# First chunk of an mLSTM and GCU kernel: the weights' bounds on GpSimd, and the first fading ahead of w_out's second pair

## The chip, the core and the metric

The kernel runs on one core of a Trainium2 chip. A core has a matrix engine (TensorE, "PE" in the profile; "PEld" is its loading of weights), three engines for elementwise work (VectorE "DVE", ScalarE "ACT", GpSimd "POOL"), a sync engine that issues transfers (SyncE "SP"), and 16 DMA engines. Each engine works through its own queue in order; between engines the order is kept by semaphores. TensorE writes to PSUM; the other operands lie in SBUF, 128 partitions wide. The metric is the device time of one execution, in microseconds; lower is better.

## What is computed

An mLSTM cell (batch 4, 8 heads, 768 steps, head size 40) gives x, 3072 tokens of 320 numbers; then a feed-forward with a cosine gate:

```python
for t in range(S):
    m_new = np.maximum(f_gate[:, :, t] + m, i_gate[:, :, t])
    f_stab = np.exp(f_gate[:, :, t] + m - m_new)
    i_stab = np.exp(i_gate[:, :, t] - m_new)
    m = m_new
    C = f_stab[..., None, None] * C + i_stab[..., None, None] * np.einsum('bhd,bhe->bhde', vt, kt)
    n = f_stab[..., None] * n + i_stab[..., None] * kt
    h_tilde = np.einsum('bhde,bhe->bhd', C, qt)
    denom = np.maximum(np.abs(np.einsum('bhd,bhd->bh', n, qt)[..., None]), 1.0)
    y[:, :, t] = 1.0 / (1.0 + np.exp(-o_gate[:, :, t])) * h_tilde / denom
x = y.transpose(0, 2, 1, 3).reshape(B * S, H * D)
h = x @ w_in                 # w_in 320 x 2048, float64
out = (h * np.cos(h)) @ w_out   # w_out 2048 x 320, float64; out is float32
```

The two weight matrices come as 64-bit floats, and the kernel turns them into 32-bit floats itself, by arithmetic on their bits.

## The kernel before

**Cells.** Time is cut into 6 chunks of 128 steps. A *cell* n = 4c + b is chunk c of batch b: the scores of keys and queries (`scores`, PE L530), their weighing with the decay (`weigh`, DVE L536), the values (`values`, PE L556 to L565), and the recurrent state st, which each cell first fades (`fade`, four POOL instructions, L650) and then increments (`state`, four DVE instructions, L692). The state is read by the values of the same cell before it is faded. The decay of a cell comes from a mask on POOL (`decay_exponents`, L434) and eight exponentials on ACT (`decay`, L448).

**Feed-forward.** It runs one chunk behind the cells, in eight blocks f2 of 2 x 128 columns of w_in. A block multiplies (`Up`, PE L715 and L709) into two PSUM banks "pup"; ACT rounds (`near`, L723), DVE subtracts (`rest`, L726), ACT takes the sine (`sin`, L731), DVE multiplies (`gate`, L735), which frees the banks for the next block. `down` (PE L829) multiplies the gated block with a *pair* of row blocks of w_out and sums up over the blocks in PSUM; it stands one block later in PE's queue.

**Conversion of the weights.** It lies wholly in the time up to and in the feed-forward's first chunk (c = 0). w_in comes in four *quarters* of three *pieces* each: two of 128 x 512 (here i0 and i1) and one of 128 x 256 (the *last*, for the tile w_in_l). w_out comes in eight *pairs* of 128 x 640, pair 0 to pair 7. For each piece or pair:

- `take_apart`, ACT: L167 makes the magnitude of the high word a float, L169 scales the low word for the rounding;
- `bound`, DVE: L173 limits the magnitude to a least and a greatest value, two operations in one instruction; L174 shifts its bits left by 5 and right by 2;
- `join`, DVE, L183: sets sign and top bit from the high word;
- `round_up`, POOL, L187: adds the low word's share.

`on_vector(made)` issues, for a list of such pieces, first all `bound`s, then all `join`s (of the first of the list last), then all `round_up`s.

**Where it stands.** The order of all queues is written out by hand. The first cells (n = 0 to 3) are done by `first_cells`, which also converts w_in's first quarter. `first_period` is cell 4 (n = B) with blocks 0 and 1 and converts pair 0, the second quarter, and pair 1. Then `both_parts(0, b)` for b = 1, 2, 3 does cells 5, 6, 7 with blocks 2b and 2b + 1. In its half i = 0 it takes apart a pair and up to two pieces (three from b = 2), converts the first two of them before `down_slot`, fades the state after the values, and converts the rest behind the fading; in its half i = 1 it converts a further pair, and at b = 1 one piece before it. In `first_period` the conversion of pair 1 (`on_vector([piece])`) stands ahead of `fade(n)` and `state(n)`.

A buffer of four quarters (`quarter()`) takes the words of w_in, three buffers `bits` those of w_out. SP's loads into them wait until the `round_up` of the piece that had the buffer before is done.

Of the kernel before, what the change touches and what calls it, by code (L numbers as in the profile page):

```python
# [16 lines left out]
OP = mybir.AluOpType  # L17
# [3 lines left out]
LEAST, GREATEST = (struct.unpack("f", struct.pack("I", b))[0] for b in (0x38000000, 0x47EFFFFF))  # L21
# [8 lines left out]
def kernel(  # L30
# [20 lines left out]
    nc = tc.nc  # L51
# [111 lines left out]
    def take_apart(dst, bits):  # L163
        n = dst.shape[1]
        hi, lo = bits[:, 0:n, 1], bits[:, 0:n, 0].bitcast(U32)

        nc.scalar.activation(out=dst, in_=hi.bitcast(FP), func=AF.Abs)  # L167

        nc.scalar.activation(out=bits[:, 0:n, 0], in_=lo, func=AF.Copy, scale=2.0 ** -29)  # L169

    def bound(dst):
        t = dst.bitcast(I32)
        nc.vector.tensor_scalar(out=dst, in0=dst, scalar1=LEAST, scalar2=GREATEST, op0=OP.max, op1=OP.min)  # L173
        nc.vector.tensor_scalar(out=t, in0=t, scalar1=5, scalar2=2, op0=OP.logical_shift_left,  # L174
                                op1=OP.logical_shift_right)

# [12 lines left out]
    def on_vector(made):  # L189

        for dst, bits in made:
            bound(dst)
        for dst, bits in (*made[1:], *made[0:1]):
            join(dst, bits)
        for dst, bits in made:
            round_up(dst, bits)
# [379 lines left out]
    def denominators(n):  # L576

        K = C // 32
        if n == B:
            d = p2.tile([128, K, 32], FP, name="dt", tag="dt")  # L580
        else:
            d = heads_of[n][:, 3].rearrange("q (k i) -> q k i", k=K)
        nc.vector.transpose(out=d, in_=heads_of[n][:, 2].rearrange("q (t k) -> q k t", t=32))
        dn = dns[n] = p2.tile([128, K, 2], FP, name="d2", tag="d2")
        both = d[:, :, FROM0:FROM1 + 1:FROM1 - FROM0]
        nc.vector.scalar_tensor_tensor(out=dn, in0=both, scalar=-TWO_PI, in1=least.rearrange("q (k g) -> q k g", g=2), op0=OP.mult, op1=OP.max)
        nc.vector.scalar_tensor_tensor(out=dn, in0=both, scalar=TWO_PI, in1=dn, op0=OP.mult, op1=OP.max)
        if n > B:
            dns[n] = d[:, :, 0:2]
        nc.vector.reciprocal(out=dns[n], in_=dn)  # L590
# [608 lines left out]
    def first_period():  # L1199
        n = B  # L1200
        up = Up(0, 0)
        scores(n)
        warm(8, psum_o())
        for e in range(2):
            up.near(e)
        for e in range(2):
            up.rest(e)
        weigh(n)
        for e in range(2):
            up.sin(e)  # L1210
            up.gate(e)
        values(n)
        seam(n)
        p, piece = outs.pop(0)
        take_apart(*piece)
        low_dimensions(n + 1)
        for some in pieces:
            take_apart(*some)
        out_of_psum(n)
        on_vector([piece])  # L1220
        up = Up(0, 1)
        turn_blocks(n + 1)
        on_vector(pieces)
        pieces.clear()
        more = weights_in(2)
        pieces.append(next(more))
        load_M(n + 2)
        pieces.extend(more)
        load_blocks(n + 2)
        load_out(p)  # L1230
        for e in range(2):
            up.near(e)
        for e in range(2):
            up.rest(e)
        for e in range(2):
            up.sin(e)
            up.gate(e)
        p, piece = outs.pop(0)
        take_apart(*piece)
        denominators(n)  # L1240
        on_vector([piece])
        fade(n)
        state(n)
        decay_exponents(n + 1)
        odd_values_of(n + 1)
        down_slot(0, 1)
        sigmoid(1)
        decay(n + 1)
        divide(n)
        scale_q(n + 1)  # L1250
        weigh_k(n + 1)
        load_G(n + 2)
        load_two(n + 2)
        load_out(p)
        load_M(n + 3)
# [6 lines left out]
    def both_parts(c, b):  # L1262

        n = (c + 1) * B + b
        cell = n < N
        for i in range(2):
            f2 = 2 * b + i
            up = Up(c, f2)
            if cell and i == 0:
                scores(n)  # L1270
            if cell and i == 1:
                if n % 2 == 1 and n > B + 1 and n + 3 < N:
                    load_two(n + 3)
            for e in range(2):
                up.near(e)
            for e in range(2):
                up.rest(e)
            if i == 0:
                if cell:
                    weigh(n)  # L1280
                    if n + 1 < N:
                        decay_exponents(n + 1)
                for e in range(2):
                    up.sin(e)
                    up.gate(e)
                if (c, b) == (0, 1):
                    seam_out(B)
                if c > 0:
                    sums(c, f2)
                if b == 0 and c == 1:  # L1290
                    sigmoid(c + 1)

                if c == 0:
                    p, piece = outs.pop(0)
                    made = [piece, *(pieces.pop(0) for _ in range(min(2 if b < 2 else 3, len(pieces))))]
                    for dst, bits in made:
                        take_apart(dst, bits)
                    on_vector(made[0:2])
                    load_out(p)
                    if b + 2 < B:  # L1300
                        load_blocks(n + 2)
                    if n in (B + 1, B + 2):
                        low_dimensions(n + 1)
                if c > 0 and cell and n + 1 < N:
                    decay(n + 1)
            else:
                if cell:
                    seam_out(n)
                if cell:
                    state(n)  # L1310
                for e in range(2):
                    up.sin(e)
                    up.gate(e)
                if c > 0:
                    sums(c, f2)
                if c == 0:
                    p, piece = outs.pop(0)
                    made = [*([pieces.pop(0)] if b == 1 else ()), piece]
                    for dst, bits in made:
                        take_apart(dst, bits)  # L1320
                    decay(n + 1)
                    sin_next()
                    on_vector(made[0:-1])
                    turn_blocks(n + 1, "k")
                    on_vector(made[-1:])
                if cell and n + 1 < N:
                    if c > 0:
                        weigh_k(n + 1)
                    odd_values(n + 1)
            down_slot(c, f2)  # L1330
            if cell and i == 0:
                values(n)
                seam(n)
                normalize_turned(n)
                fade(n)
                if c == 1 and b < 3:
                    weight_sums(b + 1)
                if n > B + 1 and n + 2 < N:
                    load_blocks(n + 2)
                if n > B + 1 and n + 3 < N:  # L1340
                    load_E(n + 3)
                if b == B - 2 and c + 2 < NC:
                    load_o(c + 2)
                if c == 0:
                    on_vector(made[2:])
                    if b + 2 < B:
                        pieces.extend(weights_in(b + 2))
                if c > 0:
                    sin_next()
            if i == 1:  # L1350
                if c == 0 and b + 2 < B:
                    load_two((n + 3) // 2 * 2)
                    load_E(n + 3)
                if c == 0:
                    turn_blocks(n + 1, "q")
                    scale_q(n + 1)
                    weigh_k(n + 1)
                    load_out(p)
                elif cell and n + 1 < N:
                    turn_blocks(n + 1)  # L1360
                    if n + 1 < (fast + 1) * B:
                        scale_q(n + 1)
                if b == B - 1 and c == fast - 1:
                    sigmoid(c + 2)
                if (c, f2) == (0, LAST):
                    weight_sums(0)
                if c == fast - 1 and b > 0:
                    up_weight_sums(b - 1)
                if c == fast - 1 and b == B - 1:
                    x_sums(c + 1)  # L1370
# [139 lines left out]
```

## Time and profile before

| what | value |
|---|---|
| three runs | 516.17, 517.38, 517.54 us; median 517.38 us |
| the profiled execution | 517.38 us; its span from the first to the last instruction is 515.5 us |
| granted clock of TensorE | 0.999 of full speed |
| busy in 60:80 us of the span | PE 17.90, DVE 15.97, ACT 14.73, POOL 13.15 us of 20 |
| busy in 80:90 us | PE 8.08, DVE 8.20, ACT 9.05, POOL 6.06 us of 10 |
| busy in 90:100 us | PE 10.00, DVE 9.69, ACT 7.17, POOL 5.27 us of 10 |
| L173, 128x640 / 128x512 / 128x256 on DVE | 480 / 464 / 337 ns each |
| L187, 128x640 / 128x512 / 128x256 on POOL | 1564 / 1309 / 745 ns each |

Times in the profile are microseconds from the start of the span, mean durations of one instruction nanoseconds. A row of the timeline has the start, the duration, the engine, the line, the operation, output and input with their shapes, how many instructions the row stands for, and in brackets how long the engine stood idle before it and what ended that. A row of the waits has the engine and line that waited, the engine, tile and line it waited for, and the microseconds in all, how often, and the longest. The first cells end, and cell 4 with the feed-forward's first block begins, at some 38 us; the second cell's values (b = 1) stand at 70 us, the third's (b = 2) at 94 us, the fourth's (b = 3) at 115.5 us; c = 0 ends at some 140 us.

### The profile page before, as it was taken

Reading aid. Unit: us, or ns where it says so; the run is one execution under the profiler, and the core shown is the slowest. Engines: PE = TensorE matmul, PEld = TensorE weight load, DVE = VectorE, ACT = ScalarE, POOL = GpSimd, SP = SyncE. Lnnn points to the kernel's source line nnn. Section 1 sums busy time; section 2 is a strip of 40 time slices with the busy share of each in tenths; the row PEclk is TensorE's granted clock in tenths of the full one; section 3 lists DMA queues with packets and bytes.
Section 4 is the critical chain, followed back from the end, with each engine's and each line's share of the span. In section 5 each row is a group of like instructions: output and inputs, shape, how many; then the busy total and the mean of one; then the engine's idle time right before and its main releaser. Section 6 shows DMA issues by size and latency. Waiting matters only on the chain.

```text
span 515.5 us, 11095 instructions
## 1 busy us (share of the span) xinstructions
PE 499.2 (97%) x4038; PEld 377.1 (73%) x4038; DVE 417.7 (81%) x839; ACT 326.4 (63%) x618; POOL 300.9 (58%) x387
## 2 busy tenths in 40 slices
PE   6999898999999999999999999999999999999997
PEld 3874454655666677778878778878878878687876
DVE  4799788988778888789987989988979867677655
ACT  2889787685945547748658867557867554443541
POOL 7525556553934855858566869656768454535340
PEclk9999999999999999999999999999999999999999
DMA  9979989998167337305728204937202000010001
GB/s 136 217 194 250 261 184 270 184 229 170 27 193 144 117 85 139 93 32 167 178 71 163 71 31 143 190 85 160 72 32 79 7 6 4 3 53 0 1 0 53
DMA packets 100903, 57.87 MB, mean 112 GB/s; under 512 B 63520, under 2 KB 93312, under 8 KB 100848
## 3 DMA queue, kind: packets, MB, share of 16 engines
q1 hardware_dynamic: 97696, 55.48, 45.9%
q10 hardware_dynamic: 2752, 1.23, 0.9%
q8 instruction: 32, 0.52, 0.4%
q0 software_dynamic: 400, 0.44, 0.3%
q14 instruction: 23, 0.19, 0.1%
HBM read 51.71 MB, written 4.11 MB: 108 GB/s over the span
## 4 chain that ended last, share of the span: by engine, by line
PE 72%; DVE 8%; DMA 6%; POOL 4%; ACT 3%; issue 3%; SPq 3%; DVEq 0%; POOLq 0%; ACTq 0%
PE acc L979 23%; PE pup L783 16%; PE pup L715 6%; PE pup L799 6%; PE late L979 4%; PE ps L530 3%; PE po L829 3%; DMA G<-G_d 2%; PE pup L709 2%; DMA blocks<-in_moe_w_in_dram 2%; PE vt L565 2%; DMA qr<-in_q_dram 2%; PE vt L556 2%; DVE t L508 1%; PE pw L1061 1%
## 5 line engine op out<-in xcount | busy, mean ns | idle before, releaser
L723 ACT ACTIVATE n<-pup 128x512 int32<-128x512 f32 x64 | 37.0, 594 | 97.6 <-DVE pup L808 65.0
L731 ACT ACTIVATE n<-n 128x512 f32<-128x512 f32 x96 | 58.2, 627 | 21.6 <-DVE n L726 15.9
L818 POOL TENSOR_TENSOR g<-g,n 128x512 f32<-128x512 f32 x31 | 39.5, 1276 | 51.4 <-ACT n L731 47.3
L726 DVE SCALAR_TENSOR_TENSOR n<-pup,n 128x512 f32<-128x512 f32 x64 | 43.1, 689 | 22.3 <-ACT n L723 19.7
L715 PE MATMUL pup<-xT,w_in_sb 128*128 128x512 f32 x128 | 58.8, 602 | 1.9 <-DVE g L735 1.7
L979 PE MATMUL acc<-w_out_sb,g 128*128 128x160 f32 x320 | 58.4, 302 | 0.0
L800 POOL TENSOR_TENSOR blocks<-blocks 128x256 f32<-128x256 f32 x32 | 25.6, 799 | 53.2 <-ACT blocks L792 53.1
L979 PE MATMUL acc<-T,g 128*128 128x160 f32 x304 | 55.8, 301 | 0.0
L448 ACT ACTIVATE E<-E,tab 128x128 f32<-128x128 f32 x160 | 50.2, 391 | 5.6 <-POOL E L434 5.4
L783 PE MATMUL pup<-xT,w_in_sb 128*128 128x256 f32 x192 | 53.1, 385 | 0.3 <-ACT blocks L792 0.2
L979 PEld LDWEIGHTS acc<-w_out_sb,g 128*128 128x128 f32 x320 | 48.9, 190 | 4.5 <-issue 2.7
L735 DVE TENSOR_TENSOR g<-pup,n 128x512 f32<-128x512 f32 x64 | 42.6, 687 | 6.1 <-ACT n L731 5.6
L715 PEld LDWEIGHTS pup<-xT,w_in_sb 128*128 128x128 f32 x128 | 23.0, 189 | 33.0 <-issue 31.2
L979 PEld LDWEIGHTS acc<-T,g 128*128 128x128 f32 x304 | 46.1, 190 | 0.9 <-issue 0.4
L783 PEld LDWEIGHTS pup<-xT,w_in_sb 128*128 128x128 f32 x192 | 33.8, 189 | 9.6 <-ACT blocks L792 5.9
L808 DVE TENSOR_TENSOR pup<-pup,blocks 128x256 f32<-128x256 f32 x32 | 13.9, 435 | 30.7 <-PE pup L799 27.5
L783 PE MATMUL pup<-x_room,room 128*128 128x256 f32 x128 | 38.2, 380 | 0.0
L791 ACT COPY blocks<-pup 128x512 f32<-128x512 f32 x32 | 18.6, 581 | 29.6 <-PE pup L783 27.8
L829 PE MATMUL po<-w_out_sb,g 128*128 128x320 f32 x128 | 36.3, 436 | 0.1
L979 PE MATMUL acc<-T,blocks 128*128 128x160 f32 x160 | 36.2, 308 | 0.0
L799 PE MATMUL pup<-xL,w_in_l 64*128 64x512 f32 x128 | 36.1, 641 | 0.0
L512 POOL TENSOR_TENSOR qG<-t,G 128x512 f32<-128x512 f32 x20 | 25.9, 1296 | 17.1 <-DVE t L508 16.9
(214 smaller groups left out, 1220.4 us busy)
## 6 DMA issues: line engine op xcount, KB each, us to landing
E<-M_d SPq DMA_DIRECT2D x21, 512.0 KB
qr<-in_q_dram SPq DMA_DIRECT2D x72, 80.0 KB
kr<-in_k_dram SPq DMA_DIRECT2D x72, 80.0 KB
bits<-in_moe_w_out_dram SPq DMA_DIRECT2D x8, 640.0 KB
G<-G_d SPq DMA_DIRECT2D x18, 256.0 KB
blocks<-in_moe_w_in_dram SPq DMA_DIRECT2D x32, 128.0 KB
out_dram<-o_sb SPq DMA_DIRECT2D x23, 160.0 KB
o<-in_o_gate_dram SPq DMA_DIRECT2D x40, 80.0 KB
```

The costliest lines, as they stand in the source:

```text
L448: nc.scalar.activation(out=Es[n][:, h], in_=Es[n][:, h], func=AF.Exp, scale=-1.0, bias=tab[:, c, 0, g:g + 1])
L512: nc.gpsimd.tensor_tensor(out=qG, in0=qkT[n][0], in1=Gs[n], op=OP.mult)
L715: nc.tensor.matmul(pu.rearrange("p (b t) -> p b t", b=B), w_in_sb[:, i, ts(2 * f2 + e, 128)], xT[c][:, i:NK * B:NK], start=(i == 0 and not ...
L723: nc.scalar.activation(out=self.n[e], in_=self.pu[e], func=AF.Copy, bias=0.25)
L726: nc.vector.scalar_tensor_tensor(out=self.n[e].bitcast(FP), in0=self.pu[e], scalar=0.25, in1=self.n[e], op0=OP.add, op1=OP.subtract)
L731: nc.scalar.activation(out=r, in_=r, func=AF.Sin, scale=TWO_PI_DOWN)
L735: nc.vector.tensor_tensor(out=g, in0=self.pu[e], in1=self.n[e].bitcast(FP), op=OP.mult)
L783: nc.tensor.matmul(bank[:, part].rearrange("p (b t) -> p b t", b=B // 2), w[:, f2], x, start=start, stop=stop, skip_group_check=True)
L799: nc.tensor.matmul(pu, w_in_l[r, f2], xL[c][r].rearrange("p b t -> p (b t)"), start=False, stop=True, skip_group_check=True)
L818: tt(out=self.g, in0=self.g, in1=self.n[e].bitcast(FP), op=OP.mult)
L829: nc.tensor.matmul(po[c][b], gs[c, f][:, ts(b, C)], w_out_sb[:, f], start=(f == 0), stop=(f == NF - 1))
L979: nc.tensor.matmul(a, lhs, rhs, start=start, stop=stop)
```

## The change

`bound` is taken in two: the limiting of the magnitude (L173) and the shift (L174), which is now `shift_out`. A new function `bounded_apart` issues `take_apart` on ACT and then the limiting on POOL. In `first_period` and in `both_parts` for c = 0 it takes the place of `take_apart`, and `on_vector` issues only the shift on DVE. The limiting thus stands in POOL's queue where `take_apart` stood in ACT's: ahead of the `round_up`s of all pieces that were taken apart together. A fourth piece (`made[3:]`, at b = 2) is taken apart and limited later, behind the fading. `first_cells` keeps `bound` on DVE for the first quarter. In `first_period`, `fade(n)` moves ahead of `on_vector([piece])` of pair 1, whose limiting still stands ahead of the fading.

```diff
     def bound(dst):
+        nc.vector.tensor_scalar(out=dst, in0=dst, scalar1=LEAST, scalar2=GREATEST, op0=OP.max, op1=OP.min)
+        shift_out(dst)
+
+    def bounded_apart(dst, bits):
+
+        take_apart(dst, bits)
+        nc.gpsimd.tensor_scalar(out=dst, in0=dst, scalar1=LEAST, scalar2=GREATEST, op0=OP.max, op1=OP.min)
+
+    def shift_out(dst):
         t = dst.bitcast(I32)
-        nc.vector.tensor_scalar(out=dst, in0=dst, scalar1=LEAST, scalar2=GREATEST, op0=OP.max, op1=OP.min)
         nc.vector.tensor_scalar(out=t, in0=t, scalar1=5, scalar2=2, op0=OP.logical_shift_left,
                                 op1=OP.logical_shift_right)
@@ on_vector
         for dst, bits in made:
-            bound(dst)
+            shift_out(dst)
@@ first_period
         p, piece = outs.pop(0)
-        take_apart(*piece)
+        bounded_apart(*piece)
         low_dimensions(n + 1)
         for some in pieces:
-            take_apart(*some)
+            bounded_apart(*some)
         out_of_psum(n)
         on_vector([piece])
...
         p, piece = outs.pop(0)
-        take_apart(*piece)
+        bounded_apart(*piece)
         denominators(n)
+        fade(n)
         on_vector([piece])
-        fade(n)
         state(n)
@@ both_parts
-                    for dst, bits in made:
-                        take_apart(dst, bits)
+                    for dst, bits in made[0:3]:
+                        bounded_apart(dst, bits)
                     on_vector(made[0:2])
...
                     for dst, bits in made:
-                        take_apart(dst, bits)
+                        bounded_apart(dst, bits)
                     decay(n + 1)
...
                 if c == 0:
+                    for dst, bits in made[3:]:
+                        bounded_apart(dst, bits)
                     on_vector(made[2:])
```

## The prediction

> **What bounds the kernel now.** First the page's busy time, which says who could be the bound, then the waits of the matrix engine (PE) in 40:215, where the change lies.
>
> ```profile
> span 515.5 us, 11095 instructions
> PE 499.2 (97%) x4038; PEld 377.1 (73%) x4038; DVE 417.7 (81%) x839; ACT 326.4 (63%) x618; POOL 300.9 (58%) x387
> ...
> PE ps L530 <- DVE st L692: 1.9, 1, 1.9
> PE pup L715 <- DVE g L735: 1.7, 2, 1.4
> PE ps L530 <- DVE t L508: 0.5, 1, 0.5
> ```
>
> PE is busy 97%: from 106 us on it hardly rests (10.00 of each 10 us up to 200), so any shift that PE has at 106 lasts to the end, and all that can be won in the first chunk is about 4 us: 1.9 (fading and state late), 1.7 (gates late), 0.5 (transposes late). Losses have no such limit. Next the timeline of 47:84, for the order in which these come about.
>
> ```profile
> 47.83 0.49 DVE L173 TENSOR_SCALAR w_out_sb<-w_out_sb 128x640 f32<-128x640 f32 x1
> 49.85 1.58 POOL L187 TENSOR_TENSOR w_out_sb<-w_out_sb,bits 128x640 int32<-128x640 int32 x1 [5.29 <-ACT kr L485]
> 52.08 0.47 ACT L167 ACTIVATE w_in_l<-blocks 128x256 f32<-128x256 f32 x1
> 53.00 3.39 PE L829 MATMUL po<-w_out_sb,g 128*128 128x320 f32 x12
> 55.21 1.28 DVE L726 SCALAR_TENSOR_TENSOR n<-pup,n 128x512 f32<-128x512 f32 x2
> 55.42 2.56 POOL L187 TENSOR_TENSOR w_in_sb<-w_in_sb,blocks 128x512 int32<-128x512 int32 x2 [3.99 <-DMA o<-in_o_gate_dram]
> 61.02 1.56 POOL L187 TENSOR_TENSOR w_out_sb<-w_out_sb,bits 128x640 int32<-128x640 int32 x1 [2.34 <-issue]
> 62.54 1.38 POOL L650 TENSOR_TENSOR st<-st,tab 40x128 f32<-40x128 f32 x4
> 63.99 1.09 POOL L434 TENSOR_SCALAR_AFFINE_SELECT E<-E 128x1024 f32<-128x1024 f32 x1
> 64.23 1.16 PE L530 MATMUL ps<-t,t 40*128 40x128 f32 x14 [1.86 <-DVE st L692]
> 82.27 1.29 DVE L735 TENSOR_TENSOR g<-pup,n 128x512 f32<-128x512 f32 x2
> 83.11 1.10 PE L715 MATMUL pup<-xT,w_in_sb 128*128 128x512 f32 x2 [1.39 <-DVE g L735]
> ```
>
> To be seen: POOL rounds up w_out's pair 0 at 49.85, 1.6 us before PE multiplies by it (53.00). The fading (L650) stands behind pair 1's rounding up, and PE waits 1.86 us for the state that follows it. And POOL's L187 mostly runs beside DVE work on PSUM (L726, L735) or transposes.
>
> The last view, the timeline of 38:42, shows what happens where it does not:
>
> ```profile
> 38.52 1.41 POOL L187 TENSOR_TENSOR w_in_sb<-w_in_sb,blocks 128x512 int32<-128x512 int32 x1 [2.08 <-DMA vs<-in_v_dram]
> 38.82 1.26 DVE L174 TENSOR_SCALAR w_in_l<-w_in_l 128x256 int32<-128x256 int32 x1
> 39.88 1.15 POOL L434 TENSOR_SCALAR_AFFINE_SELECT E<-E 128x1024 f32<-128x1024 f32 x1
> 40.11 1.19 DVE L183 SCALAR_TENSOR_TENSOR w_in_l<-blocks,w_in_l 128x256 int32<-128x256 int32 x1
> ```
>
> The same L174 takes 0.29 at 53.46, the same L183 0.42 at 54.27. Beside a POOL instruction each lasts until POOL's ends, and POOL's next one lets DVE go first: the engines take turns, one instruction each. This concerns the shift (L174) and the join (L183), both with SBUF operands only.
>
> The Trainium skill ("SBUF — State Buffer", Who interferes with whom) has this as an exclusive lock on a port pair, held for a whole instruction against a DVE operation in a two-port mode or with two SBUF inputs; the rows agree. It speaks against the change: without it the sum below would be the first rival's.
>
> **Price of a bound on POOL.** No two-operation TENSOR_SCALAR runs on POOL in the trace. Nearest row with one input: AFFINE_SELECT, 1112 ns at 1024 columns and 293 ns at 128, so 0.91 ns a column: 0.76 us for 640, 0.64 for 512, 0.41 for 256. Below: MEMSET, 621 ns at 640, 418 at 384, 737 at 768, so 0.62/0.52/0.31. Above: L187, two inputs, 1.56/1.31/0.75. I take AFFINE_SELECT, as it too reads one tensor and writes one. In all 17 instructions move (8 of w_out, 6+3 of w_in): DVE loses 8 x 0.48 + 6 x 0.42 + 3 x 0.29 = 7.2 us (L173 where no POOL instruction lies beside it), POOL gains 8 x 0.76 + 6 x 0.64 + 3 x 0.41 = 11.1 us. After 106 us both lie under PE.
>
> **First period (a).** POOL's queue now has pair 0's bound, the three bounds of w_in's second quarter (i0, i1, last), and only then pair 0's rounding up. The last bound waits for ACT's L167, which ends at 52.55; with 0.41 the rounding up can't start before 53.0 nor end before 54.55. That alone is 1.6 us on PE, which stands at 53.00 with nothing else queued. Turns add to it. DVE: pair 0's shift at 48.65 (bound 47.85 to 48.61) in place of 48.36, so the transposes end at 52.0. Bound i1 holds to 52.33, shift i0 to 52.75, bound last to 53.16, shift i1 to 53.6, rounding up of pair 0 to 55.15, shift last to 55.45, joins (0.61+0.34+0.68) to 57.1. So PE's L829 goes from 53.0 to 55.2 (+2.2), and DVE's L726 from 55.21 to 57.1 (+1.9), with gates and L167 of pair 1 (57.85 to 59.7) behind it.
>
> **First period (b), the fading.** Rounding up the quarter (55.42 to 58.68, 3.26 long) ends at 57.1+3.26 = 60.4. Then bound of pair 1 to 61.15, and the fading, now ahead, from 61.15. The shift (0.49) and join (0.82) of pair 1 fall into its four instructions, so it ends near 63.5, the state near 64.5. PE's L530, shifted by 2.2 from 61.99, would come at 64.2: the 1.86 us are used up by (a), and the scores end 0.3 later than before. What is late next is the mask L434: 60.4 + 0.76 + 1.38 + 1.56 + turns 0.49 + 0.82 = 65.4 against 63.99, +1.4. Queued behind it are eight exponentials (65.12 before), L723, L726, the weighing L536 and PE's L556, which came at 70.04 just behind the weighing (69.29, first half 0.68) and L829. So +1.4 for PE. DMA issues on POOL (L674) move along; SP's loads wait for buffers that come free as much later as PE runs, and I add nothing.
>
> **Second cell (b = 1).** From the end of the gates at 71.77 (T): bounds at T, T+1.3 and, for i1, T+2.4, each behind its L167. Shift i0 ends at T+2.4, where bound i1 competes with the join: join of pair 2 ends at T+4.5, T+3.6 before. Taken out later is i1's L173 (0.58) less a turn: L726 at 80.18 comes 0.5 later, so the gate and PE's L715 (83.11, which waits for it) too. Behind it last's shift waits 0.7 for bound of pair 3 (cover: L173s of 0.29 and 0.48 gone), +0.1 at 88.36. Together +0.6.
>
> **Third cell (b = 2).** PE has slack up to 105.48. The last piece's bound is put behind the fading (99.69, 1.70 long). Join of pair 4 ends 0.4 later by the same competition; rounding up 1.56+1.30, fading, bound 0.41, and then shift, two joins: L726 at 103.3, 102.55 before; L735 and PE's L715 +0.7. Fourth cell: two bounds of pairs, rounding up at 117.25 for use at 122.43, cover 3.6 us; nothing.
>
> **Sum**: 1.4 + 0.6 + 0.7 = +2.7. The profiled execution took 517.38 (span 515.5 and 1.9 around it), which is also the median of the runs; 517.4 + 2.7 = **520.1**. With the low price each stage loses some 0.3 less (519.2). With the high one: in (a) the rounding up ends at 56.3 and the joins at 58.2, L434 starts at 67.3 (+3.3); second cell: bounds end at T+4.2, joins T+5.7, less 0.6: +1.5; third +2.0: 524.2.
>
> A page's figure: the Trainium skill ("GPSIMD Engine Reference", Performance versus the Vector engine) puts a one-input body of at most two operations at 1.03 cycles an element, by which an estimate of 640 columns at 1.2 GHz is 0.55 us without dispatch; it would lie near the low price.
>
> **Rivals.** *Faster, by turns that cost nothing*: the bounds run in POOL's gaps (idle 44.6 to 49.85 and 51.4 to 55.4) and DVE's shifts and joins keep their 0.43 and 0.69. Then pair 0's rounding up ends at 54.6 (PE +1.6), the fading at 60.4, the 1.86 is gone (-0.3), and DVE, lighter by 1.5 us from 71.77 on, takes the 1.39 at 83.11 and the 0.53 at 88.36: -2.2, 515.2. For: the gaps are there, and L692 and L726 are not held. Against: the rows at 38.82 and 40.11. It decides if L726 of the second block comes no later than 55.5. *No change*: turns cost only half, and (a) is paid for by the 1.86 and half of DVE's relief: 517.4. *Dear bounds*: 524.2, for: POOL's two-input rows; against: AFFINE_SELECT and COPY. That the bounds don't move is excluded by the changed program's queues: 17 L173 are gone from DVE and stand on POOL.
>
> **How the numbers follow.** Forecast 0.50 (519.0 to 521.5), faster 0.20, no change 0.15, dear 0.15. Within 0.3% is +-1.55 us, about what a measurement of this kernel can tell from none. Faster 0.20, same 0.15, slower 0.65. The range runs from the faster rival's time to the dear bounds': 515.2 to 524.2.
>
> **What would show it.** POOL's TENSOR_SCALAR of 640 columns near 0.76 us where alone; PE's first L829 at about 55 with a wait for POOL; the wait of L530 for the state gone; shifts and joins with means above 0.43 and 0.69; a mask at 65.4; PE's wait for g at 83 and 105 kept or longer. Wrong, if L829 comes near 54.6 and DVE's L726 at 55.2, or if the wait at 83 vanishes.

## The result, and the profile after

| | before | after |
|---|---|---|
| median | 517.41 us (4 runs, 516.17 to 517.54) | 529.71 us (4 runs, 528.23 to 530.96) |
| ratio, 95% interval | | 1.0242 [1.0205, 1.0279] |
| profiled execution, its span | 517.38, 515.5 us | 530.77, 529.0 us |

The change makes the kernel 2.4% slower, some 12.3 us, where 2.7 us were forecast; 529.7 lies outside the range. First the page of the kernel after, its span and busy times:

```profile
span 529.0 us, 11092 instructions
PE 505.5 (96%) x4038; PEld 382.0 (72%) x4038; DVE 418.3 (79%) x822; ACT 326.5 (62%) x618; POOL 335.1 (63%) x404
```

VectorE has 17 instructions fewer and is no less busy (418.3 us, 417.7 before): its shifts alone grew from 9.5 to 14.1 us (w_out, w_in and last pieces together), probably because some of them now lie beside GpSimd's work. GpSimd has 17 more and 34.2 us more busy time, 2.0 us for each new instruction. The groups by form (line, engine, operation, shapes, count, then busy time and mean ns of one, then the idle time before them and what ended it) show the new instruction, now L178, and two that answer to it, the shift L182 and the down L837:

```profile
L178 POOL TENSOR_SCALAR w_out_sb<-w_out_sb 128x640 f32<-128x640 f32 x8 | 18.8, 2345 | 9.0 <-ACT w_out_sb L167 5.4 <-DVE g L743 3.4
L178 POOL TENSOR_SCALAR w_in_l<-w_in_l 128x256 f32<-128x256 f32 x3 | 3.2, 1065 | 0.1
L182 DVE TENSOR_SCALAR w_out_sb<-w_out_sb 128x640 int32<-128x640 int32 x8 | 5.5, 683 | 11.9 <-POOL w_out_sb L178 11.9
L837 PE MATMUL po<-w_out_sb,g 128*128 128x320 f32 x128 | 40.5, 474 | 7.0 <-POOL w_out_sb L195 7.0
```

To be seen: a bound of 640 columns lasts 2.35 us on GpSimd (0.48 on VectorE), one of 256 columns 1.07 us; the shifts of w_out wait 11.9 us for bounds, and the downs wait 7.0 us for w_out's rounding up (L195), for which they waited 0.1 us before. The waits of TensorE in 40:230 us:

```profile
PE po L837 <- POOL w_out_sb L195: 7.0, 2, 4.1
PE pup L723 <- DVE g L743: 2.5, 2, 1.7
PE ps L538 <- DVE t L516: 1.5, 2, 1.1
PE pup L717 <- POOL w_in_l L195: 0.9, 2, 0.6
```

The forecast's one certain gain is there: the 1.9 us for the state are gone from this list. But the wait of the second row, for the gates, has grown (2.5, and 1.7 in the same stretch of the kernel before, 40:215), as has that for the transposes (1.5, 0.5 before) and for w_in (0.9, 0.3 before), and a new one of 7.0 us stands at the top. Where its two parts arise, from the timeline (44:72 us, and the last row from the second cell):

```profile
49.79 2.36 POOL L178 TENSOR_SCALAR w_out_sb<-w_out_sb 128x640 f32<-128x640 f32 x1 [3.37 <-ACT w_out_sb L167]
...
52.45 4.04 POOL L178 TENSOR_SCALAR w_in_sb<-w_in_sb 128x512 f32<-128x512 f32 x2 [0.30 <-ACT w_in_sb L167]
...
56.46 1.06 POOL L178 TENSOR_SCALAR w_in_l<-w_in_l 128x256 f32<-128x256 f32 x1
...
57.49 1.55 POOL L195 TENSOR_TENSOR w_out_sb<-w_out_sb,bits 128x640 int32<-128x640 int32 x1
57.55 1.64 DVE L182 TENSOR_SCALAR w_in_l<-w_in_l 128x256 int32<-128x256 int32 x1 [0.42 <-POOL w_in_l L178]
...
59.09 7.37 PE L837 MATMUL po<-w_out_sb,g 128*128 128x320 f32 x16 [4.05 <-POOL w_out_sb L195]
...
86.27 4.57 PE L837 MATMUL po<-w_out_sb,g 128*128 128x320 f32 x16 [2.96 <-POOL w_out_sb L195]
```

Read GpSimd's rows downwards: pair 0's bound ends at 52.15, and its shift and join on VectorE take 1.6 us more. But the three bounds of w_in's quarter stand between in GpSimd's queue and take 5.1 us; the rounding up starts at 57.49, and TensorE, which has nothing else queued, waits 4.05 us. The shift of the last piece (57.55), 0.29 us where nothing lies beside it, lasts 1.64, until just after the rounding up ends (59.04).

One thing in these times is not the change's. In this profile the granted clock of TensorE fell to 0.50 in 25:30 us, where both kernels' programs are the same, and the first cell's values stand at 48.13 in place of 46.26. These 1.9 us belong to that execution: the same dip is in three of the profiles below, that of the kernel before with its fading moved among them. (In these four profiles the first cell's values stand at 48.13 to 48.26, in the eight others, that of the kernel before among them, at 45.23 to 46.57.) Less this dip, the later points of the timeline stand behind before's as follows: first down +4.2 us, values of b = 1 +4.4, values of b = 2 +9.6, end of the span +11.6. So the first period costs 4.4 us, the second cell 5.2, the third 2.0, and what TensorE has lost by then it keeps to the end. The 12.3 us between the medians have part of this dip in them; by this profile the change itself costs some 11.6.

### The profile page after: what moved, and what is told of

Read it like the earlier page. It is cut to its first block, busy times and chain, and to the rows that moved or that the text cites. A ratio compares the mean times of both kernels' runs of the same rounds, so it can differ in the third digit from the quotient of the medians.

```text
span 529.0 us, 11092 instructions
## 1 busy us (share of the span) xinstructions
PE 505.5 (96%) x4038; PEld 382.0 (72%) x4038; DVE 418.3 (79%) x822; ACT 326.5 (62%) x618; POOL 335.1 (63%) x404
## 4 chain that ended last, share of the span: by engine, by line
PE 64%; DMA 10%; POOL 8%; SPq 5%; ACT 4%; DVE 4%; issue 4%; ACTq 0%; DVEq 0%; POOLq 0%
PE acc L987 21%; PE pup L791 15%; PE pup L723 6%; PE pup L807 5%; PE late L987 4%; DMA E<-M_d 3%; PE po L837 3%; PE ps L538 2%; DMA blocks<-in_moe_w_in_dram 2%; PE pup L717 2%; PE vt L573 2%; DMA vs<-in_v_dram 2%; PE vt L564 2%; POOL w_in_sb L178 1%; SPq L381 1%
## 5 line engine op out<-in xcount | busy, mean ns | idle before, releaser
L723 PE MATMUL pup<-xT,w_in_sb 128*128 128x512 f32 x128 | 58.8, 602 | 2.8 <-DVE g L743 2.5
L734 DVE SCALAR_TENSOR_TENSOR n<-pup,n 128x512 f32<-128x512 f32 x64 | 43.1, 689 | 19.6 <-ACT n L731 17.2
L723 PEld LDWEIGHTS pup<-xT,w_in_sb 128*128 128x128 f32 x128 | 23.1, 190 | 33.6 <-issue 28.9
L837 PE MATMUL po<-w_out_sb,g 128*128 128x320 f32 x128 | 40.5, 474 | 7.0 <-POOL w_out_sb L195 7.0
L837 PEld LDWEIGHTS po<-w_out_sb,g 128*128 128x128 f32 x128 | 26.3, 209 | 20.8 <-POOL w_out_sb L195 8.7
```

Source lines behind the costliest of these rows:

```text
L723: nc.tensor.matmul(pu.rearrange("p (b t) -> p b t", b=B), w_in_sb[:, i, ts(2 * f2 + e, 128)], xT[c][:, i:NK * B:NK], start=(i == 0 and not ...
L734: nc.vector.scalar_tensor_tensor(out=self.n[e].bitcast(FP), in0=self.pu[e], scalar=0.25, in1=self.n[e], op0=OP.add, op1=OP.subtract)
L837: nc.tensor.matmul(po[c][b], gs[c, f][:, ts(b, C)], w_out_sb[:, f], start=(f == 0), stop=(f == NF - 1))
```

## Experiments

The times of the kernel before in the four series were 516.84, 516.86, 516.73 and 516.93 us; each ratio is against its own series.

### What a bound costs on GpSimd, alone

A kernel of its own, with none of the model's work: tiles of 128 to 1024 columns, two instructions of each kind in a row on GpSimd (the loops are shortened here).

```diff
+for n in (128, 256, 512, 640, 1024):
+    g.tensor_scalar(out=a[:, 0:n], in0=a[:, 0:n], scalar1=0.25, scalar2=4.0, op0=OP.max, op1=OP.min)
+for n in (256, 640):
+    g.tensor_scalar(out=a[:, 0:n], in0=a[:, 0:n], scalar1=0.25, scalar2=None, op0=OP.max)
+    g.tensor_scalar(out=a[:, 0:n], in0=a[:, 0:n], scalar1=1.0, scalar2=0.0, op0=OP.mult, op1=OP.add)
+    g.tensor_tensor(out=a[:, 0:n], in0=a[:, 0:n], in1=b[:, 0:n], op=OP.add)
+    g.tensor_copy(out=a[:, 0:n], in_=b[:, 0:n])
```

> A kernel that computes nothing of the reference: it runs rows of single GpSimd instructions alone, then six bounds of 640 columns beside six shifts on VectorE; its output is left at zero but for one copied row block. Price theory: the bound with maximum and minimum takes 3.3 ns a column plus about 0.2 us (from 2.35 us at 640 and 1.07 at 256 in the changed kernel) also where it runs alone, so 0.64, 1.07, 1.9, 2.35 and 3.6 us at 128, 256, 512, 640, 1024; one operation instead of two about half of the slope. Rival, contention: alone it takes near 0.76 us at 640 as AFFINE_SELECT's rows give, and only beside VectorE's work 2.35.

Groups by form of this kernel (L27 max and min, L30 max alone, L33 multiply and add):

```profile
L27 POOL TENSOR_SCALAR a<-a 128x640 f32<-128x640 f32 x2 | 4.7, 2340 | 0.2
...
L30 POOL TENSOR_SCALAR a<-a 128x640 f32<-128x640 f32 x2 | 3.6, 1804 | 0.2
...
L33 POOL TENSOR_SCALAR a<-a 128x640 f32<-128x640 f32 x2 | 1.4, 724 | 0.2
```

The 2.34 us are the price of the operation itself, with VectorE idle: the same form of instruction with multiply and add takes 0.72 us, and so does a copy. (From one start to the next it is 2.43 against 0.81 us.) From 256 to 640 columns max and min cost (2340 - 1061) / 384 = 3.33 ns a column, max alone (1804 - 846) / 384 = 2.5, multiply and add (724 - 404) / 384 = 0.83. The Trainium skill ("GPSIMD Engine Reference", Performance versus the Vector engine) gives one rate for bodies of up to two operations, 1.03 cycles an element, and calls one-input work roughly line-rate (Engine selection); multiply and add and the copy agree, maximum and minimum don't, and the measurement decides.

A second part was to set six bounds beside six shifts. The shifts ran much earlier than these bounds, so that it says nothing of turns; these are measured below.

### The same queue, a quarter of the columns

```diff
-        nc.gpsimd.tensor_scalar(out=dst, in0=dst, ...)
+        part = dst[:, 0:dst.shape[1] // 4]
+        nc.gpsimd.tensor_scalar(out=part, in0=part, ...)
```

> The changed kernel with the bound on GpSimd done on the first quarter of each piece's columns only (three quarters of the limiting are left out), all else in place. Price theory: a bound of 160 columns takes about 0.74 us, the price that the prediction took for 640, so the time is near the predicted 520.1 (518.5 to 522). Rival, place: what costs is that the bounds stand ahead of the roundings in GpSimd's queue and take turns with VectorE, whatever their length: 525 or more.

517.55 us (10 runs), ratio 1.0013 [0.9998, 1.0028]. Three quarters of each piece's limiting are left out. A bound of 160 columns lasts 745 ns, nearly what the prediction assumed for 640, and in place of +2.7 us there are +0.7 (-0.1 to +1.4). That is far from the rival's 525, but also below the 518.5 to 522 that were expected from the price. So a wrong price is not the whole of it: at the assumed price the sum was too large.

### No bounds at all

```diff
-        nc.gpsimd.tensor_scalar(out=dst, in0=dst, scalar1=LEAST, scalar2=GREATEST, op0=OP.max, op1=OP.min)
```

> The changed kernel without the limiting on GpSimd (left out altogether for the pieces that the change moved), so VectorE keeps its relief of 17 instructions and GpSimd pays nothing. Price theory: at or below the kernel before, 514.5 to 517. Rival, the fading's new place or the later take_apart of the fourth piece does part of the harm: 519 or more.

513.24 us (4 runs), ratio 0.9925 [0.9901, 0.9949], a little under the 514.5 to 517 expected. The limiting of all pieces but those of the first quarter is left out. Fewer instructions on VectorE and the fading's new place are together worth 0.75%, some 3.9 us; this is what the change could have won if the bounds had cost nothing on GpSimd.

### The fading's new place alone

The kernel before, with one line moved:

```diff
         denominators(n)
+        fade(n)
         on_vector([piece])
-        fade(n)
         state(n)
```

> The kernel before with only the fading of the first period moved ahead of pair 1's conversion; all bounds stay on VectorE. Theory: the wait of the scores for the state (1.86 us) goes, and the mask comes no later, since its queue holds the same work: 515.5 to 516.5. Rival: the rounding of pair 1 and the mask behind it become the next wait and nothing is won: 517 to 518.

516.06 us (12 runs), ratio 0.9976 [0.9961, 0.9992]. Better by some 1.2 us and not by the whole 1.86: the state is no longer waited for, and the fading fills time in which GpSimd had waited for pair 1's join, so that the mask comes 1.1 us earlier (64.79 less the dip of 1.9, against 63.99). But TensorE, now sooner there, waits 1.5 us ahead of the values; the last experiment shows that it is the mask, still behind the rounding up, that is waited for.

### The bounds of the first period alone, and of the later cells alone

A second argument of `on_vector` puts the bounds back on VectorE. In the one kernel it is given in `both_parts`, in the other in `first_period`:

```diff
@@ both_parts, first kernel (and so for its other pieces)
-                        bounded_apart(dst, bits)
-                    on_vector(made[0:2])
+                        take_apart(dst, bits)
+                    on_vector(made[0:2], True)
@@ first_period, second kernel (and so for its other pieces)
-        bounded_apart(*piece)
+        take_apart(*piece)
-        on_vector([piece])
+        on_vector([piece], True)
```

> The changed kernel with the bounds on GpSimd in the first period only (pair 0, second quarter, pair 1); from the second cell on they are back on VectorE. Theory of length: what is lost up to the second cell's values (76.3 against 70.0 us, of which 1.9 lie ahead of the change) stays, the rest goes: 521 to 522.5. Rival, one late stage makes the others late: above 525.

> The changed kernel with the first period's bounds back on VectorE (the fading stays ahead) and those from the second cell on still on GpSimd. Theory of length: about 7 us lost there (13.5 at the end, 6.3 at the second cell's values) less the 1 us that the fading wins: 522 to 524.5. Rival: without the first loss the later stages have cover: below 519.

First period alone 520.99 us (4 runs), ratio 1.0085 [1.0056, 1.0114]; later cells alone 524.03 us (4 runs), 1.0144 [1.0114, 1.0175]. The shares add up, 0.85% + 1.44% = 2.3%, against 2.4% for the whole. (Both kernels have the fading's new place, -0.24% by itself; without it the bounds alone are worth 1.1% and 1.7%, and the whole with the fading counted once comes to 2.5%.) By the profile of the first, the one long wait for the rounding up, 4.1 us, lies in the first period; in the second the waits are 3.0 us for the rounding up, 3.3 for the gates (1.7 before) and 1.1 for transposes (0.5 before). So the larger part of the loss lies in the second and third cell, where the prediction had the smaller one (1.3 of 2.7 us).

### Keeping TensorE's clock up

In the profile after, TensorE stands idle for 4 us ahead of the first down; the granted clock is 0.79 in 55:60 and 0.52 in 60:65, and the down takes 7.37 us in place of 4.47. To see whether that clock is part of the loss, 14 matmuls whose results nobody reads were put ahead of it:

```diff
         scale_q(n + 1)
+        warm(14, psum_o())
         down_slot(0, 1)
```

> The changed kernel with 14 matmuls of zeros, whose results nobody reads, put into TensorE's queue ahead of the first down, where TensorE stood idle for 4 us. Theory of the clock: the granted clock fell to half for the first down because TensorE had stood idle; with the gap filled the first down takes 4.5 in place of 7.4 us, and the time is 2 to 3 us below the changed kernel's 529.7. Rival: the clock falls in any case, or what it costs is won back at the next wait: 529 to 531.

529.15 us (4 runs), ratio 1.0243 [1.021, 1.0276]; 1.0242 without. The first down now took 4.57 us at full clock, and nothing was won: TensorE waited 1.6 us at the values instead, which stood 28.2 us after the first cell's as in the kernel after. So this fall of the clock, which stands right behind the wait, was no loss of its own; GpSimd's queue set the time. The second cell shows the same. In the kernel after, its scores and down at 98.20 and 99.60 take 1.47 and 5.90 us (clock 0.89 in 95:100, 0.77 in 100:105), in place of 1.16 and 4.57: 1.6 of its 5.2 us. Here they take 1.16 and 4.57, and an earlier down is slow instead (83.66: 7.46 us, clock 0.77 in 80:85 and 0.55 in 85:90). The values of b = 2 then stand 1.6 us sooner after the first cell's (55.7 in place of 57.3), yet TensorE waits 3.3 us for gates after that and the span ends no sooner. So how the loss divides between the second and the third cell depends in part on where the clock falls; its sum doesn't.

### Pair 0's rounding up ahead of the quarter's bounds

```diff
         low_dimensions(n + 1)
+        on_vector([piece])
         for some in pieces:
             bounded_apart(*some)
         out_of_psum(n)
-        on_vector([piece])
```

> The changed kernel with pair 0's conversion put ahead of the second quarter's bounds in the first period: its rounding up no longer stands behind three bounds of 2.0, 2.0 and 1.06 us in GpSimd's queue; all 17 bounds stay on GpSimd at their price. Theory of the queue's place: the 4.05 us that TensorE waits at the first down (59.09) go, and the first down starts less than 1 us behind the kernel before (53.0, plus the dip at the start where a profile has it); but the quarter's bounds now end later, so w_in's joins, and the gates of the second pair of blocks with them, come as late as they were, and most of the 4 us come back as waits for g or for w_in; left over is a gain of 1 to 3 us: 526 to 528.5 us. If the first period's loss were the place alone, all of its +4.1 us would go: 525.5. Rival, GpSimd's sum of work: the first period can't shorten whatever the order, 529 to 530.

530.18 us (4 runs), ratio 1.0269 [1.0232, 1.0306]: no gain at all. The timeline shows why (this profile has no dip; its cell's values stand at 45.23, 1.0 us ahead of before's):

```profile
52.38 4.57 PE L837 MATMUL po<-w_out_sb,g 128*128 128x320 f32 x16 [0.25 <-POOL w_out_sb L195]
...
56.05 1.06 POOL L178 TENSOR_SCALAR w_in_l<-w_in_l 128x256 f32<-128x256 f32 x1
...
58.90 1.28 DVE L734 SCALAR_TENSOR_TENSOR n<-pup,n 128x512 f32<-128x512 f32 x2
...
61.12 1.44 PE L723 MATMUL pup<-xT,w_in_sb 128*128 128x512 f32 x2 [4.17 <-DVE g L743]
```

The wait at the first down fell from 4.05 to 0.25 us, as the place in the queue would have it. But the last bound now ends at 57.11, VectorE does the three joins behind it before it comes to L734 at 58.90, and the next block waits 4.17 us for its gates. My expectation of 526 to 528.5 was wrong, and the rival right: GpSimd's sum of work is what is late, and this order only chooses who waits for it.

### The fading put back

```diff
         denominators(n)
-        fade(n)
         on_vector([piece])
+        fade(n)
         state(n)
```

> The changed kernel with the fading put back behind the second pair's conversion; all 17 bounds stay on GpSimd. Theory: with dear bounds GpSimd's queue ends the first period, and the fading ahead of the pair's rounding up still saves the wait for the state; behind it the state would come 2 to 4 us later and TensorE would wait for it at L538: 530.5 to 532.5 us. Rival: the place of the fading is worth nothing here, since the mask that follows both comes at the same time, 529 to 530. Third: the rounding up of the pair is what is late, and putting it first is faster: under 528.5.

529.48 us (4 runs), ratio 1.0236 [1.0212, 1.0259], not to be told from the kernel after. The wait for the state came back (1.3 us), the values of b = 1 stood 2.1 us later after the first cell's than in the kernel after, and at the end of the span that had shrunk to some 0.5 us (527.6, against 529.0 less the dip of 1.9). The 530.5 to 532.5 us expected were wrong; the time is the rival's, but not for its reason, since the mask and the values did come later. With dear bounds the later queue of GpSimd takes up nearly all that is won or lost here.

### Turns, measured

A kernel of its own again, the order written out: shifts (L39) and joins (L42) of 640 columns on VectorE, alone and beside GpSimd's bounds (L30), multiply-and-adds (L33) and roundings up (L36).

```diff
+beside(None, 0, shifts, 4)
+beside(None, 0, joins, 4)
+beside(bounds, 3, shifts, 6)
+beside(bounds, 3, joins, 6)
+beside(scales, 6, shifts, 6)
+beside(rounds, 4, shifts, 6)
+beside(rounds, 4, joins, 6)
```

> Micro kernel with none of the model's work; it measures how long a VectorE shift (L39) and join (L42) of 640 columns last alone, and beside GpSimd's bounds (max/min, 2.35 us), multiply-and-adds (0.72 us) and roundings up (1.56 us). Alone: shift 0.49, join 0.82 us. The prediction's theory of turns, one instruction each: a shift or join beside any of them lasts until GpSimd's instruction ends, beside a bound up to 2.35 us, and the n-th starts with GpSimd's n-th. Rival, from the changed kernel's rows (a shift of 0.90 in place of 0.49 beside a bound that lasted 1.5 us beyond it): beside max/min a VectorE instruction is delayed by about 0.4 us only, and several of them run beside one bound; beside a rounding up or a multiply-and-add it is held to that instruction's end.

Rows of its timeline for the shifts, each row a whole series of instructions:

```profile
5.04 2.08 DVE L39 TENSOR_SCALAR d<-d 128x640 int32<-128x640 int32 x4
...
12.15 4.30 DVE L39 TENSOR_SCALAR d<-d 128x640 int32<-128x640 int32 x6 [0.82 <-POOL d L45]
12.22 7.94 POOL L30 TENSOR_SCALAR b<-b 128x640 f32<-128x640 f32 x3
...
30.13 5.33 POOL L33 TENSOR_SCALAR b<-b 128x640 f32<-128x640 f32 x6
30.20 5.61 DVE L39 TENSOR_SCALAR d<-d 128x640 int32<-128x640 int32 x6 [3.32 <-POOL d L45]
...
36.55 6.74 POOL L36 TENSOR_TENSOR h<-h,e 128x640 int32<-128x640 int32 x4
36.62 8.08 DVE L39 TENSOR_SCALAR d<-d 128x640 int32<-128x640 int32 x6 [0.81 <-POOL d L45]
```

A shift alone takes 2.08 / 4 = 0.52 us. Beside three bounds all six shifts are through in 4.30 us, at 16.45, while the second bound lasts until 17.73; single ones last 0.49 or 0.89 us. Beside roundings up they go one for one: each of the first four lasts 1.70 to 1.81 us, until 0.35 us after the end of GpSimd's instruction (1.53 to 1.66), and the last two, with GpSimd done, 0.5 each. Beside multiply-and-adds likewise (0.89 each, GpSimd's 0.84). Joins do the same: four alone take 3.41 us, six beside bounds 5.91, six beside four roundings up 10.46, the first four of these 2.03 to 2.14 each. So the prediction's turns are real for roundings up, and for bounds they don't exist: a bound of max and min lets VectorE pass with a delay of at most 0.4 us an instruction (and itself gets longer, three in 7.94 us in place of 7.0). The Trainium skill ("SBUF — State Buffer", Who interferes with whom) has a lock for the whole instruction; the rows beside L33 and L36 agree with it, those beside L30 don't.

### The change at the price that was assumed

Each of the 17 instructions in its place and at full width, but as multiply by 1 and add 0:

```diff
-        nc.gpsimd.tensor_scalar(out=dst, in0=dst, scalar1=LEAST, scalar2=GREATEST, op0=OP.max, op1=OP.min)
+        nc.gpsimd.tensor_scalar(out=dst, in0=dst, scalar1=1.0, scalar2=0.0, op0=OP.mult, op1=OP.add)
```

> The changed kernel with each of the 17 instructions on GpSimd kept in its place and at its full width, but multiplying by 1 and adding 0 in place of max and min; so the limiting itself is left out of these pieces. By the micro kernel such an instruction lasts 0.72 us at 640 columns and 0.40 at 256 (so about 0.6 at 512), nearly what the prediction assumed of a bound (0.76, 0.64, 0.41), and a VectorE shift beside it is held to its end, which it is not beside max and min. So this run is the prediction's sum with the right price. The prediction's theory, price and turns: +2.7 us on the kernel before, 519 to 521 us, first down some 2.2 us and the mask some 1.4 us later than before. Rival, from the quarter-width bounds (0.75 us at 160 columns, +0.7 us): the queue's place costs 1.6 to 1.8 us at the first down, the wait for the state pays most of it back, and turns cost next to nothing on the way: 516.5 to 518 us. If turns were the loss and not the price, it would stay above 523.

518.67 us (12 runs), ratio 1.0029 [1.0011, 1.0047], +1.5 us (+0.6 to +2.4): between the two expectations. The limiting of these pieces is left out. This is the prediction's sum with the price it assumed (728 ns at 640 columns, 789 at 512, 471 at 256), so its steps can be read one by one: first the group of its 640 columns, then rows of the timeline (values of the first cell at 46.13, before 46.26):

```profile
L178 POOL TENSOR_SCALAR w_out_sb<-w_out_sb 128x640 f32<-128x640 f32 x8 | 5.8, 728 | 11.0 <-ACT w_out_sb L167 6.0 <-DVE g L743 3.4 <-DMA o<-in_o_gate_dram 1.6
...
54.66 4.57 PE L837 MATMUL po<-w_out_sb,g 128*128 128x320 f32 x16 [1.61 <-POOL w_out_sb L195]
56.21 1.28 DVE L734 SCALAR_TENSOR_TENSOR n<-pup,n 128x512 f32<-128x512 f32 x2
...
64.00 1.29 POOL L442 TENSOR_SCALAR_AFFINE_SELECT E<-E 128x1024 f32<-128x1024 f32 x1
```

The first down comes 1.7 us later than before, L734 1.0, the mask not at all. 1.0242 less 1.0029 is 2.1%: of the change's 12.3 us some 11 come with max and min in place of multiply and add, all else alike. The two differ in price and in how VectorE gets past them (turns, above); since max and min hold VectorE up less, the loss is their price.

### A version that beats both kernels

The kernel before, bounds on VectorE, with the fading and the next cell's mask ahead of pair 1's conversion, so that neither stands behind its rounding up:

```diff
         denominators(n)
-        on_vector([piece])
         fade(n)
-        state(n)
         decay_exponents(n + 1)
+        on_vector([piece])
+        state(n)
```

> The kernel before with the first period's fading and, new, the next cell's mask ahead of pair 1's conversion; all bounds stay on VectorE. With the fading alone the values of the second cell waited 1.5 us, and the chain ahead of them begins with the mask behind pair 1's rounding. Theory: the mask comes 1.5 us earlier and this wait goes for the most part: 1 us less than the fading alone, 514.5 to 515.3. Rival: pair 1's rounding, now last, holds the second down instead, and the time stays at 516.

514.45 us (7 runs), ratio 0.9952 [0.9934, 0.997]. The values of b = 1 come at 68.69, 1.4 us earlier than before, without a wait; at the second down 0.7 us are waited for pair 1's rounding up, which is now last.

## Why the prediction was wrong

**What bounds the kernel: right.** What TensorE has lost in the first chunk lasts to the end: scores of b = 3 at 123.50 against 110.04, +13.5 us with the dip, and the span +13.5.

**Price of a bound on POOL: the step that failed.** It took 0.76 us for 640 columns from AFFINE_SELECT; measured are 2.35 us (1.95 for 512, 1.07 for 256). The error lies before the arithmetic: the bracket was made of rows with other operations, as if the number of inputs set the price, and its upper end, the two-input L187 at 1.56 us, was below the truth, so that not even the dear rival's 524.2 held the time. No row of the trace before has a maximum or minimum on GpSimd; VectorE's own 0.48 us for it says nothing of GpSimd's. In all, 17 bounds cost 8 x 1.59 + 6 x 1.31 + 3 x 0.66 = 22.6 us of GpSimd more than was assumed, about half of which shows at TensorE. Of the +12.3 us, +1.5 belong to the change at the assumed price (2.7 were forecast) and some 11 to the price. The prediction's own sum, 2.7 us at 0.76 and 6.8 at 1.56, drawn on in a straight line to 2.35 gives +10.8, an estimate: with the right price it would have come near, though with another division between the cells.

**First period (a): the mechanism right, the size set by the price.** The rounding up behind four bounds is what TensorE waits for. With the assumed price the place was to cost 1.6 us and the turns 0.6 more; with multiply-and-adds the down came at 54.66, the place's 54.55 almost exactly, and the turns added 0.1. With the true price the same queue ends at 59.04 (57.2 less the dip), +4.2.

**First period (b), the fading: half right.** The wait for the state went in the kernel after, with the fading alone, and with multiply-and-adds. By the prediction's own terms the fading ends at 61.15 + 1.38 + 0.49 + 0.82 = 63.8, not near 63.5; the mask's 65.4 is added up rightly. That mask was to be late next by 1.4 us; at the assumed price it came at 64.00, as before, since L734 and the joins were 0.9 us earlier than reckoned and the turns of pair 1's shift and join cost 0.8 us (the fading takes 2.14 in place of 1.38), not 1.3. TensorE's values stood 0.2 us later than before, not 1.4.

**Second cell b = 1 and third cell b = 2.** With multiply-and-adds the second cell cost nothing (+0.6 forecast; scores at 88.52 against 88.36 with values already 0.2 late; the down came 0.8 us later, at 77.95, and the wait for gates behind it shrank from 1.39 to 0.83), and the third +0.7 (forecast +0.7; L723 at 106.31 against 105.48, less 0.16). With max and min the two cost 5.2 and 2.0 us; for the dear bounds 1.5 and 2.0 were forecast. What was not foreseen is that in the second cell the two-piece queue at i = 0 no longer fits: three bounds there take 6.1 us (78.04 to 84.14), and a down waits 2.96 us for the rounding up behind them. The rounding up itself starts only at 84.67, when pair 2's join is done, which stands last on VectorE behind i0's shift (82.30) and join; that shift had waited for the second bound.

**The rivals.** The faster one, turns that cost nothing, was half true: beside bounds they cost next to nothing, and VectorE's relief is real, 3.9 us with the fading, 2.7 if its 1.2 are taken off. But it would have fallen at the assumed price too: the quarter-wide bounds have that price and these light turns, and measured +0.7 us, not -2.2. The first down waited 1.6 us there, as this rival had said, but the waits for the gates, which were to go, stayed (1.9 us, 1.7 before), and 1.2 us were waited ahead of the values. "Dear bounds" had the right mechanism and too low a price.

## What to carry to other kernels

The price of an elementwise instruction on GpSimd goes by its operation too, not by its inputs alone: measure the very operation before moving it, and without that leave the upper end of its price open. When an engine's queue grows by more than its slack within a period, reordering may only move the wait to another place (here 4.05 us for the rounding up became 4.17 us for the gates). An instruction that an idle matrix engine waits for belongs ahead of all that only the next block needs; here that alone, fading and mask ahead of a conversion, was worth 0.5%.

## What the runs showed of the hardware that was not expected

- On GpSimd maximum and minimum cost 3.33 ns a column for the two, 2.5 for the maximum alone, against 0.83 for multiply and add.
- Beside GpSimd's max and min, VectorE's shifts and joins pass with at most 0.4 us of delay each; beside an integer add or a multiply-and-add they go one for one. Why the one gives way and the others don't is open.
- In the first micro kernel a bound of 512 columns lasted 9.57 us, beside a VectorE fill of 128 x 7680 (6.46 us) and shifts, though it had started first; 1.91 us lie on the line through the other widths. Bounds of 128 and 256 columns beside fills of 128 x 1024 (0.91 us) were on that line (0.63 and 1.06 us). It was seen once, and why is open.
- In some executions (4 of the 12 profiles of the whole kernel) the granted clock of TensorE is 0.50 in 25:30 us though it is busy 5.00 of these 5 us; the first cell's values then come 1.9 us later than in the kernel before. It is there in kernels with and without the change.
